# Twenty-one TensorE products with unread results, placed between the output projection and the last MLP weights of a one-token decode kernel

## The chip, the cores and the metric

The kernel runs on one core of a Trainium2 chip. The metric is device time in microseconds (us) of one execution; lower is better. The core has five engines with instruction streams of their own: TensorE (PE in the profile, PEld for its weight loads), VectorE (DVE), ScalarE (ACT), GpSimd (POOL) and SyncE (SP), which here only issues transfers. They meet through semaphores. Transfers from the chip's memory (HBM) run on 16 DMA engines. TensorE runs at a granted clock that the profile records: 1.00 is full, 0.50 half.

## The reference, cut to what matters

One token `x` of 512 values goes through a pre-norm attention block with a cache of 16,384 positions (32 query heads on 8 key/value heads of width 128), and then through block B, of which the part that works here is a pre-norm MLP from 512 to 1792 and back.

```python
q = (x @ wq).reshape(B, Sq, Hq, Dh)...
scores = einsum("bhqd,bhkd->bhqk", q, k) * Dh ** -0.5
p = softmax(scores)
o = einsum("bhqk,bhkd->bhqd", p, v)
A = o.reshape(B, Sq, Hq * Dh) @ wo
...
h = x + A                                  # attention with its residual
...                                        # block B on layernorm(h)
x1 = x + hs
h2 = gelu(layernorm(x1) @ w3) @ w4
return x1 + h2                             # and the outer residual: h + (x1 + h2)
```

Block B first mixes its sequence by shifts of one and two positions. With a sequence of one token every shifted quarter is the padding, so `hs` is zero and `w1` and `w2` don't enter.

## The kernel before, in words

The caches dominate: 8 heads x 2 x 4 MB of keys and values stream through on-chip buffers (`kb`, two of them for keys; `vb`, three for values), with SP issuing the transfers in the order of the program. In a loop over the 8 key/value heads, VectorE turns the keys (L390), TensorE makes the scores (L399), VectorE finds the maximum (L407), ScalarE the exponentials (L425), TensorE turns the weights (L435) and multiplies them with the values (L455); L464 and L467 gather a head's output into `A_ps`.

Around the last head SP issues the rest of the weights in order: W_o in four pieces (`WO`, by rows r: 0 to 9, 10 to 19, 20 to 27, 28 to 31), W3 in two (`W3`, chunks k: 0 to 2, 3) and W4 in four (`W4`, chunks m: 0 to 4, 5 to 8, 9 to 11, 12 and 13). W3 and W4 go into the second key buffer. Each piece has its own semaphore, and the first product that uses it waits for that.

Behind the loop comes the tail:

- L520 to L527 (VectorE): the attention output is divided by the softmax's denominators and becomes `o_b`.
- L528, L533 (TensorE): the residual `x`, then W_o: 32 rows r of four products each, four column groups of the array (32 columns each) side by side, all adding up in `O_ps[0]`.
- `row_sums` (L258 to L266): VectorE takes sums and sums of squares of the row and turns it (`hT`); TensorE's L264 adds the sums over partitions; VectorE copies the result to `st`.
- L540 (VectorE): `hc`, the row less its mean. L546 (TensorE): W3, four chunks k of four products each.
- `variance`, `seeds`, `inverse_root`: some 15 small instructions on VectorE (and, for the other root, GpSimd) that make the inverse deviation, with which ScalarE's GELU (L558) scales its input; L562 (VectorE) turns the result into `hcol`, in two halves.
- L567 (TensorE): W4, 14 chunks m of four products each, into `n_ps`.
- L571 (VectorE): `fin`, the sum with the residuals. L573 (SP): the store.

A small recorder (`Program`) keeps each engine's instructions in the order in which they are written, and finds the waits from what each reads (`r`), writes (`w`) and which PSUM bank it uses (`bank`). Nothing is reordered: an instruction that waits holds up everything behind it on its engine.

Of the kernel before, what the change touches and what calls it, by code (L numbers as in the profile page):

```python
# [122 lines left out]
W4 = ((0, 5), (5, 9), (9, 12), (12, 14))  # L123
# [8 lines left out]
def bass_sequential_preLN__gqa_block_cached__mixer_s_mlp__decode_kernel(  # L132
# [13 lines left out]
    with ExitStack() as ctx:  # L146
# [16 lines left out]
        ident = sb("ident", [128, 128], BF16)  # L163
# [20 lines left out]
        p_sb = sb("p_sb", [128, 1024 + 64], BF16)  # L184
# [24 lines left out]
        O_ps = [ps(f"O_ps{i}", [128, 512], FP32) for i in range(2)]  # L209
# [26 lines left out]
        def dve(fn, r=(), w=(), bank=()):  # L236
            return P.op("DVE", fn, r, w, bank)
# [7 lines left out]
        def pe(fn, r=(), w=(), bank=()):  # L245
            return P.op("PE", fn, r, w, bank)

        def piece(cuts, m):
            return [lo <= m < hi for lo, hi in cuts].index(True)

        def copies(col, n):

            return col.to_broadcast([col.shape[0], n])

        def row_sums(i, row, key):


            dve(lambda e: e.tensor_scalar(hr[:, :], row[:, 0:128], 0.0, 0.0, ALU.add, ALU.add,  # L258
                                          accum_out=rs[i][:, 0:1]), r=[key], w=["hr", ("rs", i, 0)], bank=[key])
            dve(lambda e: e.scalar_tensor_tensor(xs[:, :], hr[:, :], 1.0, hr[:, :], ALU.mult, ALU.mult,  # L260
                                                 accum_out=rs[i][:, 1:2]), r=["hr"], w=["xs", ("rs", i, 1)])
            dve(lambda e: e.transpose(hT[:, :, :].rearrange("p k u -> p (k u)"),
                                      hr[:, :].rearrange("p (i k) -> p k i", k=NCH)), r=["hr"], w=["hT"])
            pe(lambda e: e.matmul(n_ps[:, 0:2], mean4[:, :], rs[i][:, :], start=True, stop=True),  # L264
               r=[("rs", i, 0), ("rs", i, 1), "mean4"], w=["n"], bank=["mn"])
            dve(lambda e: e.tensor_copy(st[i][:, 0:2], n_ps[:, 0:2]), r=["n"], w=[(("st", i), 0)], bank=["mn"])  # L266

        def variance(i):

            s, S = st[i], ("st", i)  # L270

            dve(lambda e: e.scalar_tensor_tensor(s[:, 2:3], s[:, 0:1], s[:, 0:1], s[:, 1:2],
                                                 ALU.mult, ALU.subtract), r=[(S, 0)], w=[(S, 2)])
            dve(lambda e: e.tensor_scalar(s[:, 3:4], s[:, 2:3], 0.0, -1.0, ALU.min, ALU.mult),
                r=[(S, 2)], w=[(S, 3)])

        def seeds(i, ns):


            s, t = st[i], sti[i]  # L280
            S, T = ("st", i), ("sti", i)
            lo, hi = min(ns), max(ns) + 1
            for n in ns:
                mul, add = (1.0 + EPS, EPS * EPS) if n else (1.0, EPS)
                dve(lambda e, n=n, mul=mul, add=add: e.tensor_scalar(s[:, 4 + n:5 + n], s[:, 3:4], mul, add,
                                                                     ALU.mult, ALU.add), r=[(S, 3)], w=[(S, 4 + n)])
            dve(lambda e: e.tensor_single_scalar(t[:, 2 + lo:2 + hi], s[:, 4 + lo:4 + hi].bitcast(I32), 1,
                                                 ALU.arith_shift_right),
                r=[(S, 4 + n) for n in ns], w=[(T, 2)])
            dve(lambda e: e.tensor_scalar(t[:, lo:hi], t[:, 2 + lo:2 + hi], -1, 1597463007,  # L290
                                          ALU.mult, ALU.add), r=[(T, 2)], w=[(T, n) for n in ns])
# [29 lines left out]
        for b in range(2):  # L321
            for e_ in range(2):
                n = 2 * b + e_
# [7 lines left out]
            r=["ident"], w=["quarter"])  # L331
        pe(lambda e: e.matmul(O_ps[0][:, 0:128], quarter[:, :, :].rearrange("p q u -> p (q u)"), x4[:, :],
                              start=True, stop=True), r=["quarter", "x4"], w=[("O", 0)], bank=[("O", 0)])
# [6 lines left out]
            r=["hT", (("st", 0), 0), (("st", 0), 6)], w=["xn"])  # L340
# [3 lines left out]
            r=["selq_f"], w=["selq"])  # L344
        dve(lambda e: e.memset(nscale[:, :], -SCALE), w=["nscale"])
        act(lambda e: e.activation(scr[0:1, 0:1], mean4[0:1, 0:1], ACTF.Exp), r=["mean4"], w=["scr"])
        for i in range(2):
# [5 lines left out]
            r=["ident_f"], w=["row32"])  # L353
        dve(lambda e: e.tensor_reduce(row4[:, :], row32[:, :].rearrange("p (a u h) -> p u h a", a=4, u=2)[:, 0, :, :], AX.X, ALU.add),
            r=["row32"], w=["row4"])
        dve(lambda e: e.tensor_reduce(maskdd[:, :], ident_f[:, :].rearrange("p (n d) -> p d n", d=4), AX.X, ALU.add),
            r=["ident_f"], w=["maskdd"])
# [3 lines left out]
            r=["row32"], w=["zo"])  # L361
# [4 lines left out]
        for h in range(HQ):  # L366
            for k in range(NCH):
# [3 lines left out]
                   r=["xn"] + [("wo", n) for n in range(len(WO))], w=["n"], bank=["mn"])  # L371
        dve(lambda e: e.tensor_copy(QT[:, :], n_ps[:, 0:HQ]), r=["n"], w=["QT"], bank=["mn"])
        for n in range(4):
            pe(lambda e, n=n: e.matmul(m_ps[:, n * HQ:(n + 1) * HQ],
                                       selq[:, n, :, :].rearrange("p a i -> p (a i)"), QT[:, :],
                                       start=True, stop=True), r=["selq", "QT"], w=["m"], bank=["mn"])
# [95 lines left out]
        for g in range(HKV + 1):  # L472
# [33 lines left out]
            if g == HKV - 1:  # L506
# [7 lines left out]
                for n, (lo, hi) in enumerate(W4):  # L514
                    load(f"w4{n}", w4_sb[:, lo:hi, :], w4_in[:, lo:hi, :], ("k", 1, 2 + n))
                act(lambda e: e.activation(scr[0:1, 1:2], mean4[0:1, 0:1], ACTF.Gelu_apprx_tanh),
                    r=["mean4"], w=["scr"])
# [8 lines left out]
            r=["o_m"], w=["o_f"])  # L526
        dve(lambda e: e.tensor_copy(o_b[:, :], o_f[:, :]), r=["o_f"], w=["o_b"])  # L527
        pe(lambda e: e.matmul(O_ps[0][:, 0:128], quarter[:, :, :].rearrange("p q u -> p (q u)"), x4[:, :],  # L528
                              start=True, stop=False, skip_group_check=True),
           r=["quarter", "x4"], w=[("O", 0)], bank=[("O", 0)])  # L530
        for r_ in range(32):
            for q in range(4):
                pe(lambda e, r_=r_, q=q: e.matmul(O_ps[0][32 * q:32 * q + 32, 0:128], copies(o_b[:, r_:r_ + 1], 32),  # L533
                                                  wqo[:, r_ * D + q * 128:r_ * D + (q + 1) * 128],
                                                  start=False, stop=(r_ == 31), skip_group_check=True),
                   r=["o_b", ("wo", piece(WO, r_))], w=[("O", 0)], bank=[("O", 0)])
        s = st[1]
        S = ("st", 1)
        row_sums(1, O_ps[0], ("O", 0))
        dve(lambda e: e.tensor_scalar(hc[:, :, :], hT[:, :, :], s[:, 0:1], None, ALU.subtract),  # L540
            r=["hT", (S, 0)], w=["hc"])


        for k in range(NCH):
            for q in range(4):
                pe(lambda e, k=k, q=q: e.matmul(s_ps[32 * q:32 * q + 32, 0, 0:FQ], hc[:, k, :],  # L546
                                                w3_sb[:, k, q * FQ:(q + 1) * FQ], start=(k == 0), stop=(k == NCH - 1)),
                   r=["hc", ("k", 1, piece(W3, k))], w=[("s", 0)], bank=[("s", 0)])
        variance(1)
        seeds(1, (0, 1))  # L550
        inverse_root(1, 1, dve)
# [2 lines left out]
            r=["hr", (S, 0), (S, 6)], w=["xs"])  # L554
        pool(lambda e: e.tensor_tensor(xsum[:, :], hr[:, :], xs[:, :], ALU.add), r=["hr", "xs"], w=["xsum"])
        for n in range(2):
# [6 lines left out]
                hcol[:, lo:hi, :].rearrange("p m u -> p (m u)"),  # L563
                hg[:, :].rearrange("p (i m) -> p m i", m=NHC)[:, lo:hi, :]), r=[("hg", n)], w=[("hcol", n)])
        for m in range(NHC):
            for o in range(4):
                pe(lambda e, m=m, o=o: e.matmul(  # L567
                    n_ps[32 * o:32 * o + 32, 0:128], hcol[:, m, :], w4_sb[:, m, o * 128:(o + 1) * 128],
                    start=(m == 0), stop=(m == NHC - 1)),
                   r=[("hcol", 2 * m // NHC), ("k", 1, 2 + piece(W4, m))], w=["n"], bank=["mn"])  # L570
        dve(lambda e: e.tensor_tensor(fin[:, :], xsum[:, :], n_ps[:, 0:128], ALU.add),  # L571
            r=["n", "xsum"], w=["fin"], bank=["mn"])
        P.op("SP", lambda e: e.dma_start(out[0, 0:1, :].rearrange("o (q j) -> (o q) j", q=4), fin[0:128:32, :]),  # L573
             r=["fin"], w=["out"], dma="out")
# [32 lines left out]
```

## Time and profile before

| what | value |
|---|---|
| time, median of 3 runs | 193.95 us (193.80 to 193.97) |
| time of the profiled execution | 194.09 us |
| its span, first to last instruction | 192.3 us |
| TensorE busy | 112.8 us (59%), 1106 products |
| VectorE busy | 120.1 us (62%) |
| ScalarE, GpSimd busy | 16.9 us, 6.6 us |
| DMA | 79.32 MB, mean 413 GB/s |
| mean granted TensorE clock | 0.761 |

The span is what the instructions cover; 1.79 us of the profiled execution's time lie outside it. The mean busy share of the DMA engines in 40 equal slices of the span, and the clock granted to TensorE, in tenths (9 is 90% or more):

```
PEclk 9999999999985695588559655975558559669555
DMA   6999999999999999999999999999999999999991
```

A slice is 4.8 us. Busy times of TensorE are modelled from records of the hardware: products overlap, and one product's duration holds the time of its passage through the array as well as that of its columns.

### The profile page before, as it was taken

The numbers are of one execution on the slowest core, as the hardware profiler recorded it, in microseconds if no ns is written. First come the engines' busy times: TensorE is split into PE (matmuls) and PEld (weight loads), VectorE is DVE, ScalarE is ACT, GpSimd is POOL, SyncE is SP. The second block draws the span as 40 slices with busy tenths as digits, with TensorE's granted clock in tenths as the row PEclk, the third lists the DMA queues.
The fourth block names the chain that finished last, engine by engine and source line by source line (L and its number), as shares of the span: only waits on it lengthen the run. The fifth ranks groups of instructions, "written<-read, shape, count | busy, mean of one in ns | idle before, by whom it ended". The sixth has DMA issues, their size and how long they took to land.

```text
span 192.3 us, 2626 instructions
## 1 busy us (share of the span) xinstructions
PE 112.8 (59%) x1106; PEld 55.9 (29%) x1106; DVE 120.1 (62%) x225; ACT 16.9 (9%) x38; POOL 6.6 (3%) x26
## 2 busy tenths in 40 slices
PE   1025045658837766774686558645785676595443
PEld 1025001242234235223422432233223422454311
DVE  4844099499349929964795369546953796303170
ACT  3000000030030030003000300030003000600010
POOL 2000000000000000000000000000000000000060
PEclk9999999999985695588559655975558559669555
DMA  6999999999999999999999999999999999999991
GB/s 232 436 429 429 433 436 426 436 441 433 406 426 464 429 392 426 477 433 392 423 447 419 429 416 433 443 433 416 447 445 412 402 429 423 426 418 421 417 376 48
DMA packets 5066, 79.32 MB, mean 413 GB/s; under 512 B 576, under 2 KB 576, under 8 KB 1344
## 3 DMA queue, kind: packets, MB, share of 16 engines
q1 hardware_dynamic: 5048, 79.17, 96.9%
q8 instruction: 8, 0.13, 0.3%
q14 instruction: 2, 0.02, 0.0%
q10 hardware_dynamic: 8, 0.00, 0.0%
HBM read 79.17 MB, written 0.00 MB: 412 GB/s over the span
## 4 chain that ended last, share of the span: by engine, by line
DMA 40%; DVE 14%; SPq 5%; issue 2%; PE 1%
DMA kb<-in_A_k_cache_dram 30%; DVE kt L390 13%; DMA kb<-in_B_w_dram 10%; SPq L216 5%; DVE mx L407 1%; PE T_ps L435 0%; DVE pt L441 0%; PE mn_ps L567 0%; DVE fin L571 0%; PE A_ps L446 0%; SPq L102 0%; DVE o_sb L464 0%
## 5 line engine op out<-in xcount | busy, mean ns | idle before, releaser
L390 DVE STREAM_TRANSPOSE kt<-kb 128x1024 int32<-128x1024 int32 x64 | 74.0, 1212 | 11.2 <-DMA kb<-in_A_k_cache_dram 11.1
L399 PE MATMUL s_ps<-kt,qb 128*32 128x512 bf16 x256 | 47.5, 556 | 32.3 <-DVE kt L390 32.3
L455 PE MATMUL O_ps<-vb,pt 128*16 128x512 bf16 x224 | 28.9, 529 | 0.0
L399 PEld LDWEIGHTS s_ps<-kt,qb 128*32 128x32 bf16 x256 | 10.6, 113 | 61.9 <-DVE kt L390 54.1
L425 ACT ACTIVATE p_sb<-s_ps,bias 128x512 bf16<-128x512 f32 x16 | 12.8, 824 | 150.1 <-PE mn_ps L419 114.1
L467 PE MATMUL A_ps<-o_sb,zo 128*128 128x128 f32 x64 | 15.7, 422 | 10.3 <-DVE o_sb L464 10.3
L441 DVE COPY pt<-T_ps 64x256 bf16<-64x256 bf16 (+2 forms) x40 | 9.8, 261 | 15.6 <-PE T_ps L435 15.2
L407 DVE TENSOR_REDUCE mx<-s_ps 128x1 f32<-128x512 f32 x16 | 10.8, 677 | 11.9 <-PE s_ps L399 9.9
L435 PE MATMUL T_ps<-ident,p_sb 128*128 128x128 bf16 x128 | 11.8, 250 | 10.9 <-ACT p_sb L425 10.9
L467 PEld LDWEIGHTS A_ps<-o_sb,zo 128*128 128x128 f32 x64 | 13.4, 310 | 11.4 <-DVE o_sb L464 11.4
L435 PEld LDWEIGHTS T_ps<-ident,p_sb 128*128 128x128 bf16 x128 | 8.9, 112 | 12.9 <-ACT p_sb L425 12.7
L455 PEld LDWEIGHTS O_ps<-vb,pt 128*16 128x16 bf16 x224 | 9.4, 114 | 9.8 <-issue 8.5
L368 PE MATMUL mn_ps<-xn,wqo 128*128 128x1 bf16 x128 | 3.6, 165 | 9.1 <-DMA wqo<-in_A_wq_dram 9.1
L412 PE MATMUL mn_ps<-ident_f,mx 128*1 128x128 f32 x32 | 7.3, 323 | 2.5 <-DVE mx L407 2.5
L464 DVE COPY o_sb<-O_ps 128x512 f32<-128x512 f32 x8 | 5.5, 691 | 4.9 <-PE O_ps L455 4.6
L431 POOL COPY p_sb<-p_sb 128x64 bf16<-128x64 bf16 x8 | 1.9, 236 | 160.7 <-ACT p_sb L425 160.7
L368 PEld LDWEIGHTS mn_ps<-xn,wqo 128*128 128x128 bf16 x128 | 3.5, 104 | 9.2 <-issue 9.2
L415 DVE TENSOR_REDUCE nm<-mn_ps 1x4 f32<-1x256 f32 x8 | 3.2, 406 | 3.7 <-PE mn_ps L412 3.7
L533 PE MATMUL O_ps<-wqo,o_b 128*32 128x128 bf16 x128 | 3.0, 253 | 3.0 <-DMA wqo<-in_A_wo_dram 1.7
L412 PEld LDWEIGHTS mn_ps<-ident_f,mx 128*1 128x1 f32 x32 | 2.3, 90 | 7.7 <-DVE mx L407 5.4
L419 PEld LDWEIGHTS mn_ps<-nm,nscale 1*128 1x128 f32 x16 | 2.5, 198 | 5.5 <-DVE nm L415 5.5
L258 DVE TENSOR_SCALAR_CACHE_REDUCE hr<-O_ps 128x128 f32<-128x128 f32 x2 | 0.6, 292 | 5.5 <-PE O_ps L533 4.8
(79 smaller groups left out, 55.9 us busy)
## 6 DMA issues: line engine op xcount, KB each, us to landing
kb<-in_A_k_cache_dram SPq DMA_DIRECT2D x8, 4096.0 KB, 26.7
vb<-in_A_v_cache_dram SPq DMA_DIRECT2D x14, 2048.0 KB, 24.4
wqo<-in_A_wq_dram SPq DMA_DIRECT2D x1, 4096.0 KB, 12.4
kb<-in_A_v_cache_dram SPq DMA_DIRECT2D x2, 2048.0 KB, 26.6
wqo<-in_A_wo_dram SPq DMA_DIRECT2D x2, 1280.0 KB, 32.8
kb<-in_B_w_dram SPq DMA_DIRECT2D x1, 1344.0 KB, 22.9
wqo<-in_A_wo_dram SPq DMA_DIRECT2D x1, 1024.0 KB, 36.2
kb<-in_B_w_dram SPq DMA_DIRECT2D x1, 640.0 KB, 24.8
```

Source lines behind the costliest of these rows:

```text
L216: P.op(by, lambda e: e.dma_start(dst, src), w=[key, *also], dma=name)
L368: pe(lambda e, h=h, k=k: e.matmul(n_ps[:, h:h + 1], wqo[:, k * HQ * DH + h * DH:k * HQ * DH + (h + 1) * DH], xn[:, k:k + 1], start=(k == 0 ...
L390: dve(lambda e, i=i, view=view: e.transpose(view(kt), view(kb[i])), r=[("k", i, n) for n in range(KPARTS)], w=[("kt", t)])
L399: pe(lambda e, g=g, half=half, n=n, ct=ct, c8=c8: e.matmul(s_ps[32 * ct:32 * ct + 32, half, :], qb[:, n, g, :, :, :].rearrange("p a u h -> ...
L407: dve(lambda e: e.tensor_reduce(mx[:, half:half + 1], s_ps[:, half, :], AX.X, ALU.max), r=[("s", half)], w=[("mx", half)], bank=[("s", half)])
L412: pe(lambda e, half=half: e.matmul(m_ps[0:1, half * 128:half * 128 + 128], mx[:, half:half + 1], ident_f[:, :], start=True, stop=True), r= ...
L425: act(lambda e, half=half, g=g: e.activation(p_sb[:, half * 512:half * 512 + 512].rearrange("p (l s x) -> p l x s", l=8, x=2), s_ps[:, hal ...
L435: pe(lambda e, w=w: e.transpose(T_ps[:, w, :], p_sb[:, w * 64:w * 64 + 128], ident[:, :]), r=[("p", w // 8), ("p", (w + 1) // 8), "ident"] ...
L441: dve(lambda e, lo=lo, w0=w0, w1=w1, l0=l0: e.tensor_copy(to[lo:lo + 64, l0:l0 + w1 - w0, :, :], of[lo:lo + 64, w0:w1, :, lo // 64, 0, :]) ...
L455: pe(lambda e, q=q, ct=ct, n=n: e.matmul(O_ps[g % 2][32 * ct:32 * ct + 16, :], pt[g % 2][:, ct, A, 4 * q:4 * q + 4, :].rearrange("p l h -> ...
L464: dve(lambda e, g=g: e.tensor_copy(o_sb[g % 2][:, :], O_ps[g % 2][:, :]), r=[("O", g % 2)], w=[("osb", g % 2)], bank=[("O", g % 2)])
L467: pe(lambda e, g=g, j=j: e.matmul(A_ps[:, 0:128], zo[:, j, 112 - 16 * g:240 - 16 * g], o_sb[g % 2][:, j * 128:(j + 1) * 128], start=False, ...
```

## The change

A helper `spin(n)` issues n products of the identity (128x128) with the first 512 columns of the softmax weights `p_sb`, into `O_ps[1]`, which nothing reads afterwards. It is called at seven places of TensorE's stream: behind W_o's rows 19, 27 and 31 (5, 1 and 2 products), behind L264 (5), behind the last product of W3 (6), and ahead of m = 9 and m = 12 of W4 (1 each). No other engine's instructions change, and no transfer.

```diff
+        def spin(n):
+
+            for _ in range(n):
+                pe(lambda e: e.matmul(O_ps[1][:, :], ident[:, :], p_sb[:, 0:512], start=True, stop=True),
+                   r=["ident", ("p", 0)], w=[("O", 1)], bank=[("O", 1)])
+
...
                    r=["o_b", ("wo", piece(WO, r_))], w=[("O", 0)], bank=[("O", 0)])
+            spin({19: 5, 27: 1, 31: 2}.get(r_, 0))
         s = st[1]
         S = ("st", 1)
         row_sums(1, O_ps[0], ("O", 0))
+        spin(5)
         dve(lambda e: e.tensor_scalar(hc[:, :, :], hT[:, :, :], s[:, 0:1], None, ALU.subtract),
             r=["hT", (S, 0)], w=["hc"])
...
                    r=["hc", ("k", 1, piece(W3, k))], w=[("s", 0)], bank=[("s", 0)])
+        spin(6)
         variance(1)
...
         for m in range(NHC):
+            if m in (W4[2][0], W4[3][0]):
+                spin(1)
             for o in range(4):
```

## The prediction

> **What bounds the kernel now.** I read the chain of waits first, because the change touches only the last 15 us and the question is what sets the end there.
>
> ```profile
> 169.94 19.49 DMA kb<-in_B_w_dram
> 189.43 0.04 issue
> 189.48 0.43 PE mn_ps L567 x5
> 189.91 0.02 issue
> 189.94 0.29 DVE fin L571
> ```
>
> Columns: start, length in us, what. From 169.94 to 189.43 the chain is one thing, the weights of the MLP on their way from memory. Behind the last piece stand 0.43 us of TensorE (the products of L567 for m = 12 and 13), 0.29 us of VectorE and the store of the result. TensorE's own waits come next, in the timeline:
>
> ```profile
> 179.42 1.04 PE L533 MATMUL O_ps<-wqo,o_b 128*32 128x128 bf16 x32 [1.50 <-DMA wqo<-in_A_wo_dram]
> 180.66 0.62 PE L533 MATMUL O_ps<-wqo,o_b 128*32 128x128 bf16 x16 [0.20 <-DMA wqo<-in_A_wo_dram]
> 184.01 1.69 PE L546 MATMUL s_ps<-kb,hc 128*32 128x448 bf16 x16 [1.40 <-DVE sti L287]
> 187.09 1.42 PE L567 MATMUL mn_ps<-kb,hcol 128*32 128x128 bf16 x36 [1.39 <-DVE hcol L562]
> ```
>
> The bracket is the idle time before the group. Each piece of weights is consumed on arrival: W_o at 179.42 and 180.66, W3 near 184.0 and 185.04, W4's later pieces near 187.88, 188.83 and 189.47. (At 184.01 the name is a VectorE instruction, but `hc` was done at 183.13; W3's first piece is what fits.) So making TensorE faster before 189.43 buys nothing: it would wait longer for the same bytes.
>
> Last the granted clock. It changes at 3.41 us steps, so I cut the span there; columns are stretch, length, busy time (and starts) of PE, PEld, DVE, ACT, POOL, then clock, DMA share, GB/s.
>
> ```profile
> 144.68:148.09 3.41, 2.00 (x26) 1.26 (x19) 0.87 (x5) 1.64 (x4) 0.24 (x1) 1.00 1.01 427
> ...
> 154.92:158.33 3.41, 2.90 (x25) 0.85 (x28) 3.41 (x4) 0.00 (x0) 0.00 (x0) 0.50 1.02 432
> 158.33:161.74 3.41, 1.85 (x28) 0.66 (x24) 2.52 (x3) 0.00 (x0) 0.00 (x0) 1.00 1.00 427
> 161.75:165.16 3.41, 1.90 (x27) 0.75 (x15) 1.27 (x4) 0.80 (x3) 0.00 (x0) 1.00 1.00 427
> ...
> 168.57:171.98 3.41, 3.31 (x24) 2.24 (x28) 0.05 (x1) 0.00 (x0) 0.00 (x0) 0.50 0.96 396
> 171.98:175.40 3.41, 2.54 (x33) 1.41 (x25) 0.85 (x2) 0.00 (x0) 0.00 (x0) 1.00 1.02 429
> 175.40:178.81 3.41, 1.30 (x80) 1.13 (x80) 1.07 (x4) 0.00 (x0) 0.00 (x0) 1.00 1.00 414
> 178.81:182.22 3.41, 1.86 (x49) 1.32 (x50) 0.85 (x5) 0.00 (x0) 0.00 (x0) 0.50 1.03 422
> 182.22:185.64 3.41, 2.01 (x18) 0.76 (x18) 2.66 (x16) 0.00 (x0) 1.39 (x5) 0.50 0.99 397
> 185.64:189.05 3.41, 1.63 (x52) 1.03 (x48) 1.25 (x3) 0.85 (x2) 1.95 (x5) 0.50 0.64 251
> ```
>
> A full-clock stretch is followed by another after 1.85 and 2.54 us of work, and by half clock after 1.90, 2.00 and 1.30; a half-clock stretch is lifted after 2.90 and 3.31, not after 1.63 to 2.24. At 178.81 the clock falls to half and stays there to the end, the last eight products included. The only thing the added products can do for the time is to keep that from happening.
>
> **The change, part by part.** It removes nothing and moves no other engine's work; by my count of the diff it adds 21 products on TensorE (5+1+2, 5, 6, 1+1; its one-line description says 22), each with its weight load, and no new wait: they read `ident` and a finished part of `p_sb` and write O_ps[1], whose last reader was waited for at L467. No DMA is issued for them.
>
> *Price of one.* The trace has none: the nearest row for length is L455, also 512 columns.
>
> ```profile
> L455 PE MATMUL O_ps<-kb,pt x20: 379/379/420, 171.9 to 172.8; 128*16 128x512 bf16 x20
> ...
> L455 PE MATMUL O_ps<-kb,pt x12: 593/629/634, 170.7 to 171.5; 128*16 128x512 bf16 x12
> ```
>
> The first is at full clock, the second at half (durations in ns, min/median/max). Single records start in fours, 0.216 us apart at full clock (172.17, 172.39, 172.61, 172.82) and 0.427 at half (171.06, 171.49, 171.92). The four share the array by columns; an added product takes the whole width, so I price it as one such four: 0.216 or 0.427 us of TensorE. Bounds: four times the pitch of the full-width 128-column transposes of L435 at half clock (0.107) gives the same 0.427; without any overlap it would be 0.379 or 0.629.
>
> *Do they fit, at full clock?* (a) Five behind the second W_o piece: its last product starts at 177.7, 5 x 0.216 ends near 178.85; the next piece comes at 179.42, 0.57 to spare. (b) One behind the third: 8 fours x 0.055 from 179.42, then 0.216, makes 180.08 against 180.66. (c) Two behind the fourth: 180.66 + 4 x 0.055 + 0.43 = 181.31; L264 behind them on TensorE waits for row sums until 182.02 now, some 0.24 earlier then (below): 0.47 to spare. If they were late, VectorE's L266, `hc` and the root would be. (d) Five behind L264: from about 182.1 to 183.2, W3 at 184.0. (e) Six behind L546: W3's second piece at 185.04, one four of 448 columns (0.19), 6 x 0.216, is 186.55 against `hcol` at 187.08, which could come 0.33 earlier: 0.2 to spare, and L567 can lose that, since it waits again at 187.88 and 188.83. (f) One each before m = 9 and m = 12: the second starts behind the products begun at 188.83, near 189.0, and is through at 189.22, 0.25 before the last piece. All at no cost on the chain, their cover being the arrival of weights; without that cover the whole would be 21 x 0.216 = 4.5 us.
>
> *Does the clock hold?* 175.40 to 178.81 has 1.30 us of work, plus 178.81 - 177.75 = 1.06 of added products: 2.36. At full clock the next three stretches get, in array time: 12 fours x 0.055 + 3 x 0.216 + a little of (a) + L264's 0.3, about 1.7; 5 x 0.216 + 4 x 0.19 + 0.3 of (e), about 2.1; 1.0 + 12 x 0.055 + 2 x 0.216, about 2.1. The record-based busy times, which count each product's tail, would read some 0.3 to 0.6 higher. Kept rows: 1.85, 2.54; lost rows: 2.00, 1.90, 1.30. But busy time does not order them alone: 144.68 was mostly transposes of 128 columns, 158.33 only products of 512, as here. I take it that the clock holds.
>
> The Trainium skill, in TensorE: Matmul & The Clock Gate, Part 1, has the gate fall back only after an idle window of about 3.4 us. By that rule the change would do nothing for the clock, because TensorE's longest rest between 175 and 189 is 1.5 us and it should never have fallen. This trace does not agree: it fell at 178.81 after a stretch with 1.30 us of work. I go by the trace.
>
> *The gain.* Only what follows 189.43 counts: eight products, two fours.
>
> ```profile
> L533 PE MATMUL O_ps<-wqo,o_b x80: 219/219/229, 176.6 to 177.7; 128*32 128x128 bf16 x80
> ...
> L567 PE MATMUL mn_ps<-kb,hcol x56: 286/314/314, 187.1 to 189.6; 128*32 128x128 bf16 x56
> ```
>
> Same shape, full and half clock. Now: first four at 189.477, second at 189.565, plus 0.314, ends 189.879: 0.402 us. At full clock (records of L533 at 176.627 and 176.693, plus 0.219): 0.285. Gain 0.117 us. VectorE and the store keep their times. Bounds: nothing, if the last stretch is cold; 0.43, the whole TensorE piece, which no clock removes.
>
> *Sum.* The profiled execution took 194.09, 1.79 of it outside its 192.3 us span; 194.09 - 0.12 = 193.97. It lay 0.14 above the median of 193.95, so carried to the median 193.83.
>
> **Rivals.**
> 1. *The clock stays at half and the added products overrun* (slower). For it: 1.90 and 2.00 were not enough elsewhere. Block (d) is the place: from 182.62, 5 x 0.427 lasts to 184.76, 0.78 past W3; L546's four fours at 0.373 to 186.25; six at 0.427 to 188.8; L567's 14 fours at 0.107 and two more at 0.427 to 191.15, plus 0.31 is 191.46 against 189.88: +1.6, 195.5. It decides only if half clock outlasts about 185.6: a stretch so full (3.2 of 3.41) is the kind that is lifted, and from full clock at 185.64 on, 186.25 + 1.3 + 1.2 = 188.75 catches up. Against it: five of the products start while the clock is still full.
> 2. *The weights land later* (slower). Instructions come over the same engines:
>
> ```profile
> q8 instruction: 8, 0.13, 0.3%
> ```
>
> 0.13 MB in 8 is 16 KB each, one for about 276 of TensorE's 2212 records; 42 records more make a ninth likely in 42/276 = 15% of cases. At 413/16 = 26 GB/s it holds one of 16 DMA engines for 0.63 us, and the last piece needs all 16: +0.63 - 0.12, 194.46. Or TensorE's reads slow the transfers: the busiest stretch moved 396 GB/s, that with 1.30 busy 414; 4% over half of 10 us would be 0.2 and eat the gain. Against: 154.92 with 2.90 moved 432.
> 3. *It doesn't do what it says*: the clock falls somewhere after 182 and the last eight products run cold, with blocks still fitting: 0.08 late at most, from (f) at 0.427 (188.83 + 0.3 + 0.43 = 189.56). 193.95 to 194.05.
> 4. *More gain*: something behind the last product shortens too: below 193.56, for which I see no row.
>
> **How the numbers follow.** Forecast 64%, rival 1 9%, rival 2 10%, rival 3 12%, rival 4 5%. About 0.2%, 0.39 us, is what a measurement of this kernel can tell from no change; the forecast's 0.06% lies inside. Faster: rival 4 and 3 of the forecast's points, 0.08. Slower: rivals 1 and 2 and one point of rival 3, 0.20. Same: 0.72. The forecast's own range is 193.65 to 193.95; the 8-in-10 range reaches to rival 2 and down to 193.60: 193.60 to 194.50, leaving out rival 1 and part of 4.
>
> **What would show it.** Right: clock 1.00 in every stretch from 172 to 190; records of the last L567 products near 219 ns; idle before each piece of weights shorter but never gone; the last weights near 189.43 and `fin` near 189.83. Wrong: half clock at 185.6 or later with no idle before L546 (rival 1); nine fetches in q8, or the last landing after 189.6 (rival 2); `fin` before 189.5 (rival 4).

## The result and the profile after

| | kernel before | changed kernel |
|---|---|---|
| median of 22 runs each | 194.04 us | 194.42 us |
| lowest, highest | 193.80, 194.27 | 193.76, 195.63 |

The ratio of the times is 1.0027, with a 95% interval of 1.0015 to 1.0040: slower, by little but clear of the noise. What stands out is the spread, 1.9 us against 0.5. The spans say more than the times: of the changed kernel's 22, thirteen lie at 191.9 to 192.5 and nine at 192.6 to 193.7 ("raised" from here on). In two of the thirteen the time lies 2.5 and 3.2 us above the span, instead of 1.8.

The execution that was profiled belongs to the thirteen (time 193.90, span 192.1). Its granted clock, cut at its own steps (stretch, length, busy time and starts of PE, PEld, DVE, ACT, POOL, clock, DMA share, GB/s):

```profile
172.17:175.58 3.41, 2.41 (x29) 1.34 (x21) 0.97 (x3) 0.00 (x0) 0.00 (x0) 1.00 1.01 423
175.58:178.99 3.41, 2.15 (x84) 1.53 (x85) 0.94 (x4) 0.00 (x0) 0.00 (x0) 1.00 1.00 413
178.99:182.41 3.42, 2.56 (x55) 1.33 (x56) 1.11 (x7) 0.00 (x0) 0.00 (x0) 1.00 1.03 421
182.41:185.82 3.41, 2.43 (x23) 0.87 (x22) 2.60 (x14) 0.36 (x1) 1.84 (x7) 1.00 0.99 402
185.82:189.23 3.41, 2.18 (x54) 1.09 (x53) 1.06 (x2) 0.49 (x2) 1.51 (x3) 1.00 0.59 231
```

The clock column reads 1.00 all the way, where it fell to 0.50 at 178.81 before. The end of its chain of waits, and the row of its W4 products (L578 is L567 of before, L254 the added products, L582 `fin`):

```profile
162.68 26.05 DMA kb<-in_B_w_dram
188.73 0.04 issue
188.78 0.35 PE mn_ps L578 x12
189.13 0.32 PE O_ps L254
189.45 0.30 PE mn_ps L578 x8
189.75 0.02 issue
189.77 0.29 DVE fin L582
```

```profile
L578 PE MATMUL mn_ps<-kb,hcol x36: 219/219/230, 187.8 to 189.5; 128*32 128x128 bf16 x36
```

In this execution the change did what the forecast said. The last weights landed at 189.38 and `fin` began at 189.77: 0.39 us, against 0.51 before (189.43 to 189.94), a gain of 0.12. The price of an added product was right too: the five behind L264 take 1.24 us, which is four pitches of 0.215 and one duration of 0.379. So the profile of the changed kernel, alone, would have confirmed the forecast. What it can't show is the other executions.

### The profile page after: what moved, and what is told of

Same layout as the page of the kernel before. It is cut to its first block, busy times and chain, and to the rows that moved or that the text cites. A ratio compares the mean times of both kernels' runs of the same rounds, so it can differ in the third digit from the quotient of the medians.

```text
span 192.1 us, 2665 instructions
## 1 busy us (share of the span) xinstructions
PE 115.4 (60%) x1124; PEld 56.3 (29%) x1127; DVE 120.1 (63%) x225; ACT 16.9 (9%) x38; POOL 6.6 (3%) x26
## 4 chain that ended last, share of the span: by engine, by line
DMA 43%; DVE 14%; issue 2%; PE 1%; SPq 1%
DMA kb<-in_A_k_cache_dram 30%; DMA kb<-in_B_w_dram 14%; DVE kt L396 13%; DVE mx L413 1%; SPq L216 1%; PE T_ps L441 0%; PE mn_ps L578 0%; DVE pt L447 0%; PE O_ps L254 0%; DVE fin L582 0%; PE A_ps L452 0%; SPq L102 0%; DVE o_sb L470 0%
## 5 line engine op out<-in xcount | busy, mean ns | idle before, releaser
L254 PE MATMUL O_ps<-p_sb,ident 128*128 128x512 bf16 x18 | 4.9, 380 | 0.3 <-issue 0.3
L425 PE MATMUL mn_ps<-nm,nscale 1*128 1x4 f32 x16 | 3.2, 270 | 1.2 <-DVE nm L421 0.9
```

What stands on the lines that cost most here:

```text
L425: pe(lambda e: e.matmul(n_ps[:, 0:REP], nscale[0:1, :], nm[0:1, :], start=True, stop=True), r=["nm", "nscale"], w=["n"], bank=["mn"])
```

## The experiments

In what follows the changed kernel's executions count together: 22 runs, 12 of the first experiment, 4 single ones. Raised spans: 13 of 38 (the expectations below, which counted 8 of 22 and 12 of 34, miss one at the border). Times more than 2.1 us above their span: 4 of 38. Of 107 executions of the kernel before that ran beside the experiments, two had a span of 192.6, none more, and none lay more than 1.9 above its span.

**1. The change again**, no edit.

> The changed kernel, unchanged, for more single times and another profile. In its first 22 runs the spans fell into two groups, 191.9 to 192.5 us (14 runs) and 192.6 to 193.7 (8). Theory A (clock): TensorE's clock steps lie differently against the program in each execution; where a step finds too little work the clock is halved in the tail and the added products, at 0.427 us instead of 0.216, overrun the weights' arrivals. Then a third to a half of the runs lie 0.6 to 1.6 us above the rest, with a mean clock near 0.775 against 0.79 to 0.81, and a profile from the upper group shows half clock between 176 and 188 us and no idle time before L554 or L578, with the last weights still landing near 189.4. Theory B (transfers): the products' reads or their instructions delay the weights; then the upper group's last weights land after 190.

Median 194.06 of 12 (193.82 to 196.12), ratio 1.0020 (1.0000 to 1.0040); four spans at 193.1 to 193.3, mean clock 0.775 to 0.784 in those, and one of these times 2.8 above its span. The profile (span 192.2, time 193.98) shows where the clock steps fall in another execution:

```profile
173.22:176.63 3.41, 1.79 (x17) 1.06 (x9) 1.53 (x5) 0.00 (x0) 0.00 (x0) 1.00 0.99 413
176.63:180.04 3.41, 2.60 (x81) 2.33 (x83) 0.39 (x2) 0.00 (x0) 0.00 (x0) 0.50 1.04 429
180.04:183.46 3.42, 3.06 (x58) 1.53 (x58) 1.06 (x6) 0.00 (x0) 0.00 (x0) 1.00 0.98 401
```

A stretch of full clock that holds two waits (for the last head's gather and for `o_b`) has 1.79 us of work; the next one is at half clock, and it holds the 80 first W_o products (2.32 us instead of 1.30) and the start of the five added ones. W_o ended at 182.16 instead of 181.02. That was caught up here. So the profile is of an ordinary execution, and which theory explains the raised ones stayed open; the mean clock does not sort them, since ordinary spans came with 0.774 to 0.814.

**2. Only the products among W_o's rows** (5, 1, 2).

```diff
-        spin(5)
-        spin(6)
-            if m in (W4[2][0], W4[3][0]):
-                spin(1)
```

> Only the eight products among W_o's rows (5, 1, 2); the 13 behind them are left out. Theory A: even at half clock they make the W_o stage end at most 0.9 us later (5 x 0.427 from 178 lasts to 180.1, then 0.86 + 0.43 + 0.43), and that is caught up, because TensorE now rests 1.4 us before W3 and 1.4 us before W4; so every run like the kernel before: 193.9 to 194.3, no upper group. Theory B: about 8/21 of the loss, an upper group some 0.4 us up.

A miss for both theories: median 194.21, ratio 1.0022 (1.0005 to 1.0038), three of 12 spans at 193.3 to 193.5, and one time 2.8 above an ordinary span. The W_o products alone can do it.

**3. Only the products behind L264 and W3** (5, 6).

```diff
-            spin({19: 5, 27: 1, 31: 2}.get(r_, 0))
...
-            if m in (W4[2][0], W4[3][0]):
-                spin(1)
```

> Only the eleven products behind L264 and behind W3 (5, 6). Without those among W_o's rows the clock falls near 178.8 as before, so Theory A has the eleven run at half clock in most runs: five to 184.8 where W3 is there at 184.0, W3's sixteen to 186.3, six more to 188.8 unless the clock is back by then; 0.5 to 1.6 us slower than before in more than half of the runs, median 194.6 or more. Theory B: 11/21 of the loss, so the median within 0.2 us of 194.1 and an upper group of the same frequency as the changed kernel's, half as high.

The other miss: no span above 192.5, so these eleven alone made none of 11 executions overrun. Its profile has the clock at half for W_o and back behind it:

```profile
173.10:176.51 3.41, 1.74 (x17) 1.06 (x9) 1.58 (x5) 0.00 (x0) 0.00 (x0) 1.00 0.98 410
176.51:179.93 3.42, 2.99 (x108) 2.75 (x112) 0.34 (x2) 0.00 (x0) 0.00 (x0) 0.50 1.04 426
179.93:183.34 3.41, 2.06 (x38) 0.93 (x27) 2.03 (x12) 0.00 (x0) 0.18 (x1) 1.00 0.99 405
```

Yet median 194.15, ratio 1.0012 (1.0000 to 1.0023): four of 11 times lie 2.5 to 2.8 us above their span. This is a second loss, outside the span.

**4. The change and eight products earlier**, in the waits at 173 and 175: three ahead of the last head's L467, written into O_ps[0], and five between L528 and L533.

```diff
+            if g == HKV - 1:
+                spin(3, 0)
...
+        spin(5)
```

> The change plus three products before the last head's gather (L475) and five before W_o, in the waits of 0.8 and 1.3 us at 173.2 and 175.3. Theory A: stretches that end between 174 and 178 then find more work, so the clock is halved less often ahead of the tail and the upper group gets smaller: under a quarter of the runs, median 193.9. If the clock isn't up yet at 173 the eight cost up to 1.3 us more, so the runs that remain in the upper group lie higher, up to 197. Theory B: 29 products instead of 21, so the loss grows by a third: upper group as frequent, median 194.5 or more.

Median 193.91 (193.71 to 194.00 in 11 runs), ratio 0.9992 (0.9983 to 1.0001). No raised span, no time more than 1.9 above its span.

**5 and 6. The length of TensorE's stream alone.** One-column products in an idle stretch near 20 us, on the kernel before: 11 (22 records; shown) and 29 (58).

```diff
+        for _ in range(11):
+            pe(lambda e: e.matmul(n_ps[:, 200:201], ident[:, :], ident[:, 0:1], start=True, stop=True),
+               r=["ident"], w=["pad"], bank=["mn"])
```

> The kernel before plus eleven one-column products in TensorE's idle time near 20 us, ahead of the scores: 22 more TensorE records, as in the run with the five and six products alone, and no work in the tail. That run had four of 11 times 0.7 to 1.0 us above the others with no longer a span, and its profile shows a ninth instruction fetch of 16 KB at 193.1, behind the span; the kernel before shows eight fetches and none of 35 times raised. Theory F (instructions): the length of TensorE's stream alone does it. Then some 3 to 5 of 11 times are raised by 0.7 to 1.0 with spans of 192.0 to 192.4, median 194.0 to 194.2. Theory A (clock alone): nothing changes, 193.85 to 194.2 in every run.

> The kernel before plus 29 such one-column products near 20 us: as many records as the run with 29 added products, which had its ninth fetch at 189.0, inside the program, and no raised time. Theory F: the fetch comes before the end and nothing waits for it: 193.85 to 194.2 in every run, nine fetches in the profile. If instead any ninth fetch costs, times up to 195. Theory A: 193.85 to 194.2, whatever the fetches. The gain of 0.12 of the run with 29 must not appear here: the clock at the end is half as before.

With 11: median 194.16, ratio 1.0019 (1.0007 to 1.0032); five of 12 times 2.4 to 2.9 above their spans, all spans 192.2 to 192.5. With 29: 194.01, ratio 0.9999 (0.9991 to 1.0008), none. The instruction queue on the two pages, each within the span:

```profile
q8 instruction: 9, 0.15, 0.3%
```

The line is the same on both; before it was 8. In the trace's records of transfers the ninth, of 16 KB, starts at 189.85 with 11 products and at 188.75 with 29. So a longer stream alone, with no work in the tail, makes the time outside the span longer in some executions: in five of 12 with 22 records more, in none of 11 with 58. That the place of the ninth fetch decides is not shown here, since the profile with 11 products is of an execution without the loss (time 194.08); the profiles of experiments 12 and 15 support it.

The profile with 29 products also shows what the kernel before does, with nothing added in the tail, when the clock falls ahead of W_o (first two rows: clock stretches; then TensorE's rows, L536 is W_o, L549 W3):

```profile
173.64:177.05 3.41, 1.48 (x13) 1.06 (x9) 1.80 (x6) 0.00 (x0) 0.00 (x0) 1.00 0.98 410
177.05:180.47 3.42, 3.18 (x112) 2.91 (x112) 0.12 (x1) 0.00 (x0) 0.00 (x0) 0.50 1.04 430
177.22 3.18 PE L536 MATMUL O_ps<-wqo,o_b 128*32 128x128 bf16 x112 [1.30 <-DVE o_b L530]
180.55 0.41 PE L536 MATMUL O_ps<-wqo,o_b 128*32 128x128 bf16 x16 [0.15 <-DMA wqo<-in_A_wo_dram]
183.90 1.68 PE L549 MATMUL s_ps<-kb,hc 128*32 128x448 bf16 x16 [1.81 <-DMA kb<-in_B_w_dram]
```

W_o runs at half clock, and TensorE still waits 1.81 us for W3: the lateness is gone by then (span 192.1).

**7. The change with a stream as long as experiment 4's** (eight one-column products more).

> The change plus eight one-column products near 20 us, so that its stream is as long as that of the run with 29 added products. Theory A: the spans still fall into two groups, 191.9 to 192.5 and, in a quarter to a half of the runs, 192.6 to 193.7, since nothing of the clock is changed; Theory F as the whole cause: no raised run, all 193.7 to 194.0. Both at work: two groups of spans, but no time more than 2.1 us above its span.

Median 194.07, ratio 1.0012 (0.9998 to 1.0025). Four of 12 spans raised (192.6 to 193.3; a fifth, which the later expectations count in, at 192.5), one time 2.2 above its span, the others at most 2.03. The loss in the span stays. The one outside is rare in this kernel, but for a single execution of experiment 15; over all kernels with 29 added or one-column products a time more than 2.1 us above its span came in 2 of 81 executions, against 14 of 73 with 8 to 21. So there are two losses with two causes.

**8. The same length without the five products behind row 19.**

```diff
-            spin({19: 5, 27: 1, 31: 2}.get(r_, 0))
+            spin({27: 1, 31: 2}.get(r_, 0))
```

> The change without the five products behind W_o's row 19, plus 13 one-column products near 20 us (as long a stream again). Theory A as the runs so far have mended it: the loss sits in those five, 2.1 us at half clock behind 80 products that themselves take 2.3 instead of 1.3; without them W_o is caught up on the arrival of its last pieces. Then no span above 192.6 and a median of 193.9 to 194.05. If the loss sits in the later blocks (five behind L264, six behind W3), as I had put it, spans of 192.6 and more remain in a quarter of the runs or more.

Median 193.90, ratio 0.9995 (0.9986 to 1.0003), spans 192.0 to 192.3 in all 11, where 13 in 38 would give about four raised ones. The loss in the span needs the five behind row 19.

**9 to 12. Single profiles of the change.**

> The changed kernel again, for a profile of an execution with a raised span (192.6 to 193.7; 12 of its 34 runs so far). Theory A: there the clock step that ends between 174.5 and 177 leaves the clock at half for two steps, W_o's first 80 products take 2.3 us and the five behind row 19 2.1, the W_o stage ends 1.5 us or more later than 181.3, and the root, GELU and W4 follow that late, with the last weights landed near 189.4 long before. Theory F inside the span: a ninth fetch of 16 KB starts before 189 and TensorE stands still with its weights landed and its input ready. With an unraised span: clock full or lifted by 180, nothing late.

> The same once more, for the same end: a raised span shows W_o's end after 182.8 with two half-clock steps before it (Theory A) or a stand-still behind a fetch (Theory F inside the span).

> The same once more, for the same end: a raised span shows W_o's end after 182.8 with two half-clock steps before it (Theory A) or a stand-still behind a fetch (Theory F inside the span).

> The same once more, for the same end: a raised span shows W_o's end after 182.8 with two half-clock steps before it (Theory A) or a stand-still behind a fetch (Theory F inside the span).

Times 194.22, 194.00, 193.92, 194.56; spans 192.0 to 192.2, so none of the raised. The fourth shows the loss outside the span: 2.56 us there, and its ninth fetch starts at 193.74, 1.7 us behind the last instruction. In experiment 3's profile it started at 193.06, 1.1 behind, and the time was not longer (193.79).

**13 to 15. Single profiles of experiment 7's kernel.**

> The change with eight one-column products near 20 us, for a profile of a raised span (five of 12 so far). Theory A: the clock is at half for the five behind row 19 and for W_o's last pieces, W_o ends after 182.5, W4 starts after 188.3, the last weights land near 189.4 and TensorE doesn't rest between W4's pieces. Theory F inside the span: W_o ends near 181 and TensorE stands still later with everything it needs there.

> The same once more, for the same end: a raised span shows W_o's end after 182.5 at half clock (Theory A) or a late standstill (Theory F inside the span).

> The same once more, for the same end: a raised span shows W_o's end after 182.5 at half clock (Theory A) or a late standstill (Theory F inside the span).

193.85 and 193.96 with ordinary spans; the third is a raised one, span 193.5, time 196.50 (its ninth fetch came at 195.28, 1.8 us behind the last instruction, and it shows the loss outside the span as well). Its clock stretches:

```profile
171.25:174.66 3.41, 3.41 (x31) 1.22 (x34) 0.00 (x0) 0.00 (x0) 0.00 (x0) 0.50 1.02 422
174.66:178.08 3.42, 1.71 (x17) 1.06 (x9) 1.61 (x5) 0.00 (x0) 0.00 (x0) 1.00 1.00 413
178.08:181.49 3.41, 3.02 (x82) 2.34 (x83) 0.31 (x2) 0.00 (x0) 0.00 (x0) 0.50 1.02 425
181.49:184.90 3.41, 3.21 (x59) 1.53 (x58) 1.08 (x6) 0.00 (x0) 0.00 (x0) 1.00 1.01 406
```

and the part of its chain of waits from W_o on, cut in the middle (start, length, what; L542 is W_o, L581 W4, L254 the added products):

```profile
178.47 2.33 PE O_ps L542 x77
180.80 1.54 PE O_ps L254 x5
182.34 0.56 PE O_ps L542 x32
182.90 0.32 PE O_ps L254
183.23 0.36 PE O_ps L542 x16
...
188.52 0.59 DVE hcol L574
189.11 0.04 issue
189.16 0.78 PE mn_ps L581 x36
189.93 0.32 PE O_ps L254
190.26 0.28 PE mn_ps L581 x12
190.54 0.32 PE O_ps L254
190.86 0.25 PE mn_ps L581 x8
191.14 0.29 DVE fin L585
```

No transfer stands in this part. Here half clock until 174.66 had already made the last head's values late, `o_b` is there at 178.42 instead of 176.57, half clock from 178.08 slows W_o, and now the added products stand on the chain: 1.54 + 3 x 0.32 = 2.50 us. The last weights landed at 189.74; without the 2.50, and at the same clock (worked out: 191.11 - 2.50 = 188.6), TensorE would have been done before that and would have waited for them. Theory A had the clock at half for W_o's last pieces too; it was back at 181.49, ahead of them. This is one execution, and of the kernel with eight one-column products more; that the other raised ones are like it is inferred.

**16. Only the five behind row 19** (and 24 one-column products).

> The kernel before plus the five products behind W_o's row 19 alone and 24 one-column products near 20 us (29 in all). Theory A: the five suffice: in a fifth to two fifths of the runs the span is raised, by 0.3 to 1.3 us, since at half clock W_o ends up to 1.9 us late and everything behind it is at half clock too; no gain in the others, since nothing holds the clock to the end. If the later blocks are needed for the loss, all spans lie at 192.0 to 192.5.

Median 194.14, ratio 1.0006 (0.9997 to 1.0015); three of 11 spans at 192.6 to 192.9, none with more than 1.9 outside. Two of the three are at 192.6, which the kernel before showed twice in 107 as well, and the interval holds 1. So the five are likely enough to raise the span, at a smaller price than with the others behind them, but this run doesn't prove it; what experiments 2 and 8 show is that they are enough together with the three behind them, and that none of 11 spans is raised without them.

**17 and 18. Can the 0.12 be had?** Experiment 4 without the products behind row 19 and those in W4 (seven one-column products fill up the length), and experiment 4 again.

> Three products ahead of the last head's gather, five ahead of W_o, then the change's 1 and 2 among W_o's rows, 5 behind L264 and 6 behind W3, without its five behind row 19 and its two in W4; seven one-column products near 20 us make up the length of the stream (29). Now that a raised span has been profiled: the added products that stood on the chain there were those behind row 19 (1.54 us), row 27 and in W4 (0.32 each). Here only 0.32 of these 2.50 are left, and the earlier products hold the clock at full for W_o. So no raised span and no time far above its span: 193.7 to 194.0, median 193.9, 0.1 below the kernel before. If the clock falls in the gap at 178, half of the last gain is lost: 193.95.

> The change plus the three and five earlier products, again, as it was the only one below the kernel before in every run. If its 193.71 to 194.0 in 11 runs was no luck: again no raised span and no time 2.1 us above its span, median 193.85 to 193.95, ratio 0.9990 to 0.9996. If the raised spans come back in a quarter of the runs, the earlier products don't hold the clock in all cases.

193.93 (193.75 to 194.36), ratio 0.9993 (0.9985 to 1.0002), one of 11 spans at 192.6, as two of the 21 of the kernel before beside it; and 193.89 (193.78 to 194.15), ratio 0.9993 (0.9984 to 1.0002), none above 192.3. The repetition's profile has its clock step at 173.25, beside the first experiment's 173.22:

```profile
173.25:176.66 3.41, 3.36 (x28) 1.73 (x21) 1.44 (x5) 0.00 (x0) 0.00 (x0) 1.00 1.01 423
176.66:180.08 3.42, 3.30 (x120) 1.97 (x117) 0.48 (x2) 0.00 (x0) 0.00 (x0) 1.00 1.02 419
```

The same stretch with 3.36 us of work instead of 1.79 is followed by full clock. Both versions are below the kernel before by about 0.07%, with intervals that just reach 1: likely better, not proven.

## Why the prediction was wrong

*What bounds the kernel, and the gain.* Right where the clock held. The profile gave 0.12 us from the last landing to `fin`, the forecast's 0.117. In 19 of 34 runs of the changed kernel, those with neither loss, the median was 193.94 against 194.03 to 194.04 before; as they are picked by their outcome, the profile is the better evidence.

*"Does the clock hold?"* This is the step that failed, and with it "All at no cost on the chain, their cover being the arrival of weights". I cut the span at the steps of one execution and added up the work in those stretches. The steps do not keep their place: in the profiles the one near the last head's values lies at 171.57, 171.98, 172.17, 173.22 and 174.66. The Trainium skill, in TensorE: Matmul & The Clock Gate, Part 1, says that the 3.4 us window runs freely and isn't reset when a kernel starts; these profiles agree, and the prediction weighed another rule of that part and passed over this one. In three profiles a stretch at full clock holds the wait before the last head's gather and 0.8 us or more of the one for `o_b` (it starts at 173.10, 173.22 and 174.66); it has 1.71 to 1.79 us of work, and the next is at half clock. That stretch lies ahead of the added products, so they can't prevent it. The margin is narrow: in experiment 11's profile a stretch from 172.86 holds 0.7 us of that wait and has 1.90 us of work, and the next is at full clock. Half clock there isn't all, since the steps at 173.10 and 173.22 raised no span; at 174.66 the last head's values were late as well. Where between them the loss begins isn't shown.

*Rival 1 was the result, with its place and its cause mis-told.* I gave overrunning at half clock 9% and put it behind L264 and W3. In experiment 3 those eleven raised no span; in its profile W_o at half clock, 2.99 us of work, was followed by full clock. The overrun starts behind row 19, ahead of all that I had worked out at half clock. I had costed the added products against weights that arrive late; in the raised execution that was profiled TensorE itself is late, by 1.85 us at `o_b`, the waits that were to hide the products are gone, and 2.50 us of them stand on the chain, where the sum had nothing. A third of the executions have such spans. The kernel before uses the same waits to catch up, as experiment 6's profile shows, and its spans hardly vary. The price, 0.5 to 1.6 us, is of the size that I gave (1.6); that is luck, for I had added it up from other blocks.

*Rival 2* happened in part, elsewhere: a ninth fetch stands in two of six profiles of the changed kernel, and the weights' landing (189.25 to 189.55 in the profiles with ordinary spans) did not move. Four of 38 executions have 0.7 to 1.4 us more outside the span; one of these was profiled, with a fetch at 193.74. That the fetch is the cause there is likely, not proven.

*The chances.* 72% for no change came from one position of the clock against the program. The range held the median of 194.42, by luck, since its upper end was made for weights that land later; and it did not hold the distribution: the single times of the 22 go from 193.76 to 195.63, and what moves the median is how often the two losses come, which no number of the prediction was made for.

## What to carry to other kernels

A wait that hides added work in the profile is also the reserve with which the kernel catches up when it is late: cost such work against the latest execution, not against the one that was profiled. A profile is one sample; where a clock that steps by itself decides, slide its steps over the program before summing, and look at the spread of single runs before the median. And count instructions: eleven products of one column, far from the tail, made five of 12 executions 0.6 to 1.1 us longer, so a control with the same count and no work belongs beside every such change.

## What the runs showed of the hardware that was not expected

- TensorE's clock steps come 3.41 us apart or at multiples of it, and their place against the program differs from execution to execution: near the last head's values it went from 171.57 to 174.66. Stretches with 1.71 to 1.79 us of work in 3.41 were followed by half clock, without a rest longer than 1.3 us in them. The work alone doesn't decide: a stretch with 1.90 kept full clock at 172.86 in experiment 11's profile, and one with 1.90 lost it at 161.75 in the kernel before.
- TensorE's instructions come in pieces of 16 KB on the queue q8: a longer stream of TensorE alone added one. At 1106 products the profile shows eight; with 8 to 21 products more a ninth started between 189.83 and 193.74 or wasn't recorded, with 29 between 188.75 and 189.33, but for one execution (195.28). The two starts 1.7 and 1.8 us behind the last instruction (193.74 and 195.28) went with 0.8 and 1.2 us more outside the span, one 1.1 behind it (193.06) and all earlier ones with none. What decides when it starts, and what waits for it behind the span, is open.
- TensorE's added reads left the transfers alone: the last weights landed at 189.25 to 189.55 in the profiles with ordinary spans, 189.43 before (189.74 in the raised one).
